# A decode kernel's tail: half rows of the result on 8 neighbouring partitions, odd weight rows summed apart, one plain store, and other cuts of the last weight load

## The chip, the cores and the metric

The kernel runs on one core of a Trainium2 chip. The metric is the device time in microseconds (us) of the whole program. The span of a trace, from the first to the last instruction, is 1.7 to 1.8 us shorter than the time of the same execution (211.0 against 212.7 for the kernel before). All positions "at 207.73" below are microseconds from the start of the span in the trace that is named.

The engines are called PE (matmul), PEld (PE's weight loads), DVE (vector), ACT (scalar), POOL and SP (which issues most of the DMAs).

## The reference

Four tokens go through a layernorm; its result feeds an attention block over a window of 2048 cached keys (16 key heads, 32 query heads of 128) and an MLP block. The results are added.

```python
xn = layernorm(A_x)                                   # 4 x 576
out = A_x + attention(xn, K, V, wq) @ wo              # wo: 4096 x 576
          + xn + gelu(layernorm(xn) @ w3) @ w4        # w3: 576 x 4608, w4: 4608 x 576
# (in the MLP block the shifted terms are zero for a sequence of one token)
```

All inputs are bf16. About 87 MB of cache and weights are read once; there is little arithmetic per byte.

## The kernel before

The result, 4 x 576, is summed in one PSUM tile `acc` in two halves of 288 columns: half `i` in the 32-partition group `i`, batch `b` at partition `32 i + 8 b`. The stationary operands (`gT`, `op`, `idz`) are 32 columns wide with zeros between the four batches. All of `x + xn`, the attention projections (`o_proj`, once per 4 heads) and the MLP's second matmul (`mlp_out`) are added into it without ever resetting it.

```python
    W4_PIECES = [0, 10, NFH, NFH + 10, NFH + 14, NF]

    def load_w4():
        t = wp.tile([P, NF, D], BF16, tag="w", name="w4_sb")
        for lo, hi in zip(W4_PIECES, W4_PIECES[1:]):
            e = lo // NFH
            src = B_w4[e * (F // 2):(e + 1) * (F // 2), :].rearrange("(p i) n -> p i n", i=NFH)
            nc.sync.dma_start(out=t[:, lo:hi, :], in_=src[:, lo - e * NFH:hi - e * NFH, :])
        w_tiles["w4"] = t
    ...
    RS = QD // B
    acc = ps_acc.tile([P, CW], F32)
    nc.vector.memset(acc[:], 0.0)
    ...
    def acc_matmuls(lhsT, rhs):
        for i in range(2):
            nc.tensor.matmul(out=acc[i * QD:(i + 1) * QD, :], lhsT=lhsT, rhs=rhs[:, i * CW:(i + 1) * CW],
                             start=False, stop=False, skip_group_check=True)
    ...
    def o_proj(h):
        if h % WOQ < WOQ - 1:
            return
        for i in range(WOR):
            acc_matmuls(op[:, i, :], wo_tiles[h // WOQ][:, i, :])
    ...
    def mlp_out(lo, hi):
        w4 = w_tiles["w4"]
        for i in range(lo, hi):
            acc_matmuls(gT[:, i, :], w4[:, i, :])
```

`w4` is issued last of all loads, so its pieces also land last. The end of the program, after the last K and V tiles (`hl` is the last head):

```python
    for s in range(NSL):
        pv(hl, s)
    o_scale(hl)
    o_turn(hl - 1)
    o_sum(hl - 1)
    pieces = list(zip(W4_PIECES, W4_PIECES[1:]))
    mlp_out(*pieces[0])
    o_turn(hl)
    o_sum(hl)
    o_spread(hl)
    o_pick(hl)
    mlp_out(*pieces[1])
    o_proj(hl)
    for lo, hi in pieces[2:]:
        mlp_out(lo, hi)

    fin = const.tile([2 * QD, CW], out.dtype)
    nc.vector.tensor_copy(out=fin[:], in_=acc[0:2 * QD, :])
    nc.sync.dma_start(out=o2.rearrange("b (i n) -> i b n", i=2), in_=fin[0:2 * QD:RS, :])
```

PE executes its instructions in this order. The first piece of `w4` stands in front of the last head's transposes (`o_turn(hl)`), and the last head's projection stands in front of the later pieces.

## Time and profile before

| what | where it is read | value |
|---|---|---|
| time | 212.67 us, median of 3 runs | 212.56 to 212.80 |
| bytes read, rate over the span | page, part 3 | 87.17 MB, 413 GB/s |
| share of DMA in the chain that ended last | page, part 4 | 67% |
| last load landed, PE, DVE, store issued | chain, timeline | 206.99, 0.68 us, 0.45 us, 208.21 |
| from the store's issue to the end of the span | 211.0 - 208.21 (spans are given to 0.1 us) | 2.79 us |

The page's slices (40 of 5.3 us each; a digit is the busy share in tenths) show the DMA engines at nine tenths or more from the second slice until the last:

```profile
PEclk9999579799859655957999669999998596969998
DMA  7999999999999999999999999999999999999990
```

The chain that ended last, in order of time (start, length, what; only its end):

```profile
180.05 26.94 DMA w_sb<-in_B_w_dram
206.99 0.04 issue
207.03 0.68 PE acc L314 x8
207.71 0.02 issue
207.73 0.45 DVE fin L601
```

So the program ends with a load, eight matmuls that were waiting for it, an eviction and the store. The timeline of the same stretch (start, length, engine, line, operation, output<-inputs, shapes, count, and in brackets the idle time before it and what ended it):

```profile
198.94 1.40 PE L314 MATMUL acc<-w_sb,gT 128*32 128x288 bf16 x20
...
200.27 0.66 PE L400 MATMUL oT<-ident_w,O_sb 128*128 128x128 f32 x4
...
201.59 1.16 PE L314 MATMUL acc<-w_sb,gT 128*32 128x288 bf16 x16
...
202.64 1.16 PE L314 MATMUL acc<-wo_sb,op 128*32 128x288 bf16 x16
...
204.27 2.04 PE L314 MATMUL acc<-w_sb,gT 128*32 128x288 bf16 x28 [0.47 <-DMA w_sb<-in_B_w_dram]
...
207.03 0.67 PE L314 MATMUL acc<-w_sb,gT 128*32 128x288 bf16 x8 [0.72 <-DMA w_sb<-in_B_w_dram]
...
208.21 0.68 SPq L602 DMA_DIRECT2D out_dram<-fin  x1
```

The first piece (rows 0 to 10 of `w4`, 20 matmuls) starts at 198.94 with no wait, the head's work fills the time until 203.8 (204.27 - 0.47), and PE then waits twice for a load. PE has slack; the loads do not.

### The profile page before, as it was taken

What the parts mean: (1) busy time and instruction counts of PE and PEld (TensorE: products, weight loads), DVE (VectorE), ACT (ScalarE), POOL (GpSimd) and SP (SyncE); (2) the same over time, 40 slices, a digit from 0 to 9 for tenths busy, and PEclk for the clock granted to TensorE, in tenths of its full rate; (3) what the DMA queues carried; (4) which work ended last, traced back from release to release, by engine and by line L of the source; (5) the groups of instructions that cost most, each with busy time, mean ns of one, the idle gap of its engine ahead of it and who ended that gap; (6) DMA issues with size and microseconds to landing.
All of it is one profiled execution on the core that took longest, in us unless ns stands there. A gap on an engine that the chain in (4) does not pass through costs nothing.

```text
span 211.0 us, 2402 instructions
## 1 busy us (share of the span) xinstructions
PE 150.4 (71%) x955; PEld 62.2 (29%) x955; DVE 121.3 (57%) x216; ACT 33.9 (16%) x63; POOL 2.8 (1%) x15
## 2 busy tenths in 40 slices
PE   0386695869395009669999499968693967898982
PEld 0122232224132003214454144334240322433561
DVE  4832989485731082825725968985867284763220
ACT  7703101021102000202121121120211020202300
POOL 4010000000000000000000000000000000000000
PEclk9999579799859655957999669999998596969998
DMA  7999999999999999999999999999999999999990
GB/s 246 435 413 441 422 441 410 443 435 413 450 419 426 438 419 429 434 444 432 416 438 435 416 427 437 435 432 424 436 426 426 420 444 435 422 429 429 425 382 30
DMA packets 6797, 87.32 MB, mean 414 GB/s; under 512 B 758, under 2 KB 770, under 8 KB 1282
## 3 DMA queue, kind: packets, MB, share of 16 engines
q1 hardware_dynamic: 6778, 87.17, 97.2%
q8 instruction: 7, 0.11, 0.2%
q14 instruction: 4, 0.03, 0.0%
q10 hardware_dynamic: 8, 0.00, 0.0%
HBM read 87.17 MB, written 0.00 MB: 413 GB/s over the span
## 4 chain that ended last, share of the span: by engine, by line
DMA 67%; PE 18%; DVE 7%; issue 4%; ACT 1%; SPq 1%; POOL 0%; POOLq 0%; DVEq 0%
DMA w_sb<-in_B_w_dram 29%; DMA vn<-in_A_v_cache_dram 26%; DMA kn<-in_A_k_cache_dram 12%; PE S L335 9%; DVE kt L215 3%; PE g_ps L453 2%; PE q_ps L277 2%; PE O L387 2%; PE oT L400 1%; PE acc L314 1%; DMA first<-in_A_x_dram 1%; DVE qz L309 1%; PE gT_ps L465 1%; DVE mx L341 1%; PE S L357 1%
## 5 line engine op out<-in xcount | busy, mean ns | idle before, releaser
L335 PE MATMUL S<-kt,qz 128*128 128x512 bf16 x256 | 82.0, 452 | 3.1 <-DVE kt L215 3.1
L215 DVE STREAM_TRANSPOSE kt<-kn 128x1024 int32<-128x1024 int32 x64 | 76.8, 1221 | 10.3 <-DMA kn<-in_A_k_cache_dram 9.4
L387 PE MATMUL O<-vn,PT 128*32 128x512 bf16 x256 | 27.8, 434 | 38.5 <-DMA vn<-in_A_v_cache_dram 36.9
L335 PEld LDWEIGHTS <-qz 128*128 128x128 bf16 x256 | 22.2, 106 | 43.2 <-issue 28.5
L363 ACT ACTIVATE E<-S 128x512 bf16<-128x512 f32 x16 | 9.5, 597 | 123.4 <-PE S L357 123.4
L387 PEld LDWEIGHTS <-PT 128*32 128x32 bf16 x256 | 7.3, 95 | 47.2 <-DVE kt L215 23.8
L369 DVE STREAM_TRANSPOSE PT<-E 128x512 bf16<-128x512 bf16 x16 | 11.4, 711 | 14.3 <-ACT E L363 14.3
L353 DVE TENSOR_REDUCE nm<-mg 8x1 bf16<-8x16 f32 x16 | 2.5, 154 | 20.3 <-PE mg L348 20.2
L394 ACT ACTIVATE O_sb<-O,rd 128x512 f32<-128x512 f32 x16 | 11.0, 687 | 16.5 <-issue 11.0
L410 DVE TENSOR_REDUCE on<-oT 128x8 bf16<-128x128 f32 x16 | 4.6, 286 | 15.7 <-PE oT L400 15.7
L400 PE MATMUL oT<-ident_w,O_sb 128*128 128x128 f32 x64 | 11.8, 315 | 0.0
L341 DVE TENSOR_REDUCE mx<-S 128x1 f32<-128x512 f32 x16 | 10.5, 658 | 1.3 <-PE S L335 1.3
L400 PEld LDWEIGHTS oT<-ident_w,O_sb 128*128 128x128 f32 x64 | 9.6, 167 | 5.4 <-issue 3.9
L357 PE MATMUL S<-nm,j_row 8*128 8x512 bf16 x16 | 6.9, 431 | 0.0
L373 PEld LDWEIGHTS dn<-rs,same_j 128*128 128x128 f32 x32 | 5.8, 188 | 2.9 <-ACT E L363 0.7
L326 PE MATMUL S<-negbig,ohT 4*128 4x512 bf16 x16 | 6.2, 385 | 0.0
L314 PE MATMUL acc<-w_sb,gT 128*32 128x288 bf16 x72 | 5.3, 287 | 1.2 <-DMA w_sb<-in_B_w_dram 1.2
L348 PE MATMUL mg<-dm,sel_jb 128*8 128x16 bf16 x16 | 2.8, 175 | 3.7 <-DVE dm L343 3.7
L348 PEld LDWEIGHTS <-sel_jb 128*8 128x8 bf16 x16 | 1.3, 83 | 12.6 <-issue 6.7
L453 PE MATMUL g_ps<-w_sb,ln2T 128*32 128x512 bf16 (+1 forms) x50 | 4.9, 443 | 0.0
L314 PE MATMUL acc<-wo_sb,op 128*32 128x288 bf16 x64 | 4.6, 287 | 0.0
L373 PE MATMUL dn<-rs,same_j 128*128 128x1 f32 x32 | 4.6, 212 | 0.0
(89 smaller groups left out, 72.8 us busy)
## 6 DMA issues: line engine op xcount, KB each, us to landing
kn<-in_A_k_cache_dram SPq DMA_DIRECT2D x16, 2048.0 KB, 22.3
vn<-in_A_v_cache_dram SPq DMA_DIRECT2D x16, 2048.0 KB, 23.9
wo_sb<-in_A_wo_dram SPq DMA_DIRECT2D x4, 1152.0 KB, 25.8
w_sb<-in_B_w_dram SPq DMA_DIRECT2D x2, 2304.0 KB, 31.4
wq_sb<-in_A_wq_dram SPq DMA_DIRECT2D x2, 2048.0 KB, 9.6
w_sb<-in_B_w_dram SPq DMA_DIRECT2D x2, 1440.0 KB, 29.2
w_sb<-in_B_w_dram SPq DMA_DIRECT2D x3, 576.0 KB, 30.5
w_sb<-in_B_w_dram SPq DMA_DIRECT2D x1, 1152.0 KB, 28.7
```

The source lines that it names most:

```text
L215: nc.vector.transpose(out=kt[:], in_=src)
L314: nc.tensor.matmul(out=acc[i * QD:(i + 1) * QD, :], lhsT=lhsT, rhs=rhs[:, i * CW:(i + 1) * CW], start=False, stop=False, skip_group_check= ...
L335: nc.tensor.matmul(out=S_ps[h][:], lhsT=qz[:, z0:z0 + P], rhs=kt[:, ib, :, e:2 * QD:2].rearrange("p c k -> p (c k)"), start=False, stop=Fa ...
L341: nc.vector.reduce_max(out=mx[:], in_=S_ps[h][:], axis=AX.X)
L357: nc.tensor.matmul(out=S_ps[h][:], lhsT=j_row[:], rhs=st.pop(("nm", h))[:, 0:1].to_broadcast([NJ, NW]), start=False, stop=False, skip_grou ...
L363: nc.scalar.activation(out=E[h][:].rearrange("p c k -> p (c k)"), in_=S_ps.pop(h)[:], func=ACT.Exp, scale=scale, accum_out=rs[:])
L369: nc.vector.transpose(out=PT[h][:], in_=E.pop(h)[:])
L373: nc.tensor.matmul(out=dn[:], lhsT=same_j[:], rhs=st.pop(("rs", h))[:], start=True, stop=True)
L387: nc.tensor.matmul(out=O_ps[h][g * QD:(g + 1) * QD], lhsT=PT[h][:, c, :], rhs=vn[:, :, c, :], start=(s == 0), stop=False, skip_group_check ...
L394: nc.scalar.activation(out=O_sb[h][:], in_=O_ps.pop(h)[:], func=ACT.Copy, scale=st.pop(("rd", h))[:, 0:1])
L400: nc.tensor.transpose(out=oT[:, s, :], in_=o[:, s, :], identity=ident_w[:, s * NJ:s * NJ + P])
L453: nc.tensor.matmul(out=g_ps[g * QD:(g + 1) * QD], lhsT=ln2T[:, k, :], rhs=rhs, start=(j == 0), stop=False, skip_group_check=True)
```

## The change

Its intent: the result's half rows (batch 0 half 0, batch 0 half 1, ...) go to 8 neighbouring partitions, so that the store is one plain 8 x 288 copy. For this the stationary operand becomes 10 columns wide with batches at columns 1, 3, 5, 7; half 0 takes columns 1 to 8 and half 1 columns 0 to 7, which shifts its rows by one partition. Both halves then land in one column group, so, to keep two groups running, the even weight rows go to group 0 and the odd ones to group 1. Group 1's sum is copied out by ACT before the last four rows, which go to group 0 alone, and DVE adds it at the end. The first half of `w4` is loaded in one piece, and the last piece is two rows instead of four.

```diff
-    W4_PIECES = [0, 10, NFH, NFH + 10, NFH + 14, NF]
+    W4_PIECES = [0, NFH, NFH + 10, NFH + 14, NF - 2, NF]
 ...
+    OR = 2 * B
+    OW = OR + 2
+    gT = cleared([P, NF, OW], "gT")
+    op = cleared([P, WOR, OW], "op")
 ...
+    def acc_matmuls(terms, nq=2):
+        for i in range(2):
+            for n, (lhsT, rhs) in enumerate(terms):
+                q = n % nq
+                nc.tensor.matmul(out=acc[q * QD:q * QD + OR, :], lhsT=lhsT[:, 1 - i:1 - i + OR],
+                                 rhs=rhs[:, i * CW:(i + 1) * CW], start=False, stop=False, skip_group_check=True)
 ...  (o_proj and mlp_out now take two rows at a time; idz, op and gT are written at columns 1:9:2)
-        for i in range(lo, hi):
-            acc_matmuls(gT[:, i, :], w4[:, i, :])
+        for i in range(lo, hi, 2):
+            acc_matmuls([(gT[:, i + u, :], w4[:, i + u, :]) for u in range(2)], 2 if hi <= NF - 4 else 1)
 ...
-    for lo, hi in pieces[2:]:
+    mlp_out(*pieces[2])
+    odd = const.tile([OR, CW], F32)
+    nc.scalar.activation(out=odd[:], in_=acc[QD:QD + OR, :], func=ACT.Copy)
+    for lo, hi in pieces[3:]:
         mlp_out(lo, hi)
 
-    fin = const.tile([2 * QD, CW], out.dtype)
-    nc.vector.tensor_copy(out=fin[:], in_=acc[0:2 * QD, :])
-    nc.sync.dma_start(out=o2.rearrange("b (i n) -> i b n", i=2), in_=fin[0:2 * QD:RS, :])
+    fin = const.tile([OR, CW], out.dtype)
+    nc.vector.tensor_tensor(out=fin[:], in0=acc[0:OR, :], in1=odd[:], op=ALU.add)
+    nc.sync.dma_start(out=o2.rearrange("b (i n) -> (b i) n", i=2), in_=fin[:])
```

PE's order is not touched: `mlp_out(*pieces[0])`, now 18 rows, still stands in front of `o_turn(hl)`.

## The prediction

> **What bounds it now.** The loads. The page's slices show the DMA engines at nine tenths or more until about 205 of 211.0 us (87 MB at 413 GB/s). The chain of waits ends: last w4 load landed 206.99, 8 PE matmuls 0.68, DVE copy of the accumulator 0.45 (starts 207.73), store issued 208.21 (issue 0.68 us), then 2.1 us to the end. The change touches only this tail; nothing before 198 us should move.
>
> **Where the w4 pieces land** (issue times plus time to landing): rows 0-10 at 198.1, 10-18 about 200.7, 18-28 at 204.2, 28-32 at 205.6, 32-36 at 207.0. In the timeline PE runs the first piece at 198.94 without waiting, then the last head's transposes (200.27), its spread (201.31), the second piece (201.59, while DVE masks and picks until 202.60), the projection (202.64), and from 203.5 waits only on loads.
>
> **What the change does.**
> 1. Rows 0-18 in one load: nothing of it is usable before about 200.7. PE's order is unchanged, so these 36 matmuls stand in front of the last head's transposes, and PE idles from 198.94 to 200.7. Their spacing in the trace is 58 ns (20 in 1.40 us, each 286 ns long). Estimate from these durations: transposes at 203.0, reduced by 204.0, rows 18-28 at 204.3, projection 205.5 to 206.45, rows 28-32 until 207.2. PE's slack is lost, and PE, not the last load, ends the chain.
> 2. New ACT copy of the odd sums, 8x288: about 0.42 us, worked out from the 128x512 copies (0.6-0.69 us). In the built program the first matmul of rows 32-34 waits for it: 207.2 to 207.7.
> 3. Rows 32-36 go to one column group only. [...] eight take 1.13 us, until 208.85. The smaller last piece would help only if the load still ended the chain.
> 4. DVE add instead of copy: 0.43-0.45, the same (a 4x576 float add took 0.73). It starts near 208.9 instead of 207.73: **+1.15 us**.
> 5. Store as 8x288 instead of 2x4x288: [...] the issue should fall from 0.68 towards the 0.33-0.58 of other issues. **-0.25 us** (estimate).
> 6. Smaller clears on ACT, seed matmuls one after the other (some 0.6 us more): off the chain, PE waits for the second layernorm until 12.3.
>
> **Sum:** 212.67 + 1.15 - 0.25 = **213.5 us**, 8 in 10 within 212.3 to 214.4. Faster by over 2%: 0.01; within 2%: 0.96; slower: 0.03.
>
> **What would show it.** Right: PE idle for 1.5-2 us near 199, waiting for a w4 load; the last chain made of PE work from about 200.8 on, with ACT's copy in it; the last load lands near 207 and nobody waits for it; DVE add near 208.9; a shorter store issue. Wrong on 1: PE's last wait is still for w4, DVE add below 208. Wrong on 3: spacing near 60 ns in rows 32-36.
>
> **What would make it wrong.** The first half landing earlier (198-199.5) as one transfer; a throttled clock in the tail after PE's idle (the trace has stretches at 0.50 after pauses), a microsecond or more; a much cheaper store; small last pieces delaying the last landing.

The 1.13 us are part of the +1.15 of step 4, and the sum came to 212.67 + 1.15 - 0.25 = 213.5 us.

## The result, and the profile after

| | before | after |
|---|---|---|
| median us | 212.70 (5 runs) | 215.33 (5 runs) |
| lowest to highest | 212.56 to 212.80 | 213.33 to 215.93 |
| all runs | | 213.33, 215.33, 215.84, 215.93, 215.00 |

The ratio is 1.0113, with a 95% interval from 1.0081 to 1.0144. (Ratios here are the mean time of one kernel's fast runs over that of the other's of the same rounds, so they are not quite the ratio of the medians.) All runs count as fast: on one core the limit for a slow run is 1.5% above the fastest, and these are 1.2% above. But the spread is new: 2.6 us where the kernel before has 0.24.

The one trace at hand was of the shortest execution, 213.33 us. Its chain (start, length, what):

```profile
171.03 29.61 DMA w_sb<-in_B_w_dram
...
200.68 2.37 PE acc L183 x36
...
204.37 2.81 PE acc L183 x42
...
207.21 0.41 ACT odd L600
...
207.66 1.16 PE acc L183 x8
...
208.91 0.45 DVE fin L605
```

The last load is no longer in it; from 200.68 on it is PE's work, with ACT's copy in the middle. The timeline of the same trace:

```profile
200.68 2.37 PE L183 MATMUL acc<-w_sb,gT 128*8 128x288 bf16 x36 [1.93 <-DMA w_sb<-in_B_w_dram]
...
202.98 0.66 PE L401 MATMUL oT<-ident_w,O_sb 128*128 128x128 f32 x4
...
204.30 1.39 PE L183 MATMUL acc<-w_sb,gT 128*8 128x288 bf16 x20
...
206.51 0.66 PE L183 MATMUL acc<-w_sb,gT 128*8 128x288 bf16 x8
...
207.66 1.14 PE L183 MATMUL acc<-w_sb,gT 128*8 128x288 bf16 x8 [0.49 <-ACT odd L600]
...
209.38 0.37 SPq L606 DMA_DIRECT2D out_dram<-fin  x1
```

Up to here every step is where the prediction had put it: the wait for the large load ends at 200.68 (foretold 200.7), ACT copies at 207.21 (207.2), DVE adds at 208.91 (208.9). Only the store is cheaper than foretold: 211.5 - 209.38 = 2.12 us from issue to end, against 2.79. So a short execution is explained, and four of the five executions are not: they are 1.7 to 2.6 us longer than this one.

### The profile page after: what moved, and what is told of

The parts are those of the page before. It is cut to its first block, busy times and chain, and to the rows that moved or that the text cites. A ratio compares the mean times of both kernels' runs of the same rounds, so it can differ in the third digit from the quotient of the medians.

```text
span 211.5 us, 2390 instructions
## 1 busy us (share of the span) xinstructions
PE 146.3 (69%) x941; PEld 61.2 (29%) x955; DVE 120.8 (57%) x216; ACT 33.9 (16%) x64; POOL 2.7 (1%) x15
## 4 chain that ended last, share of the span: by engine, by line
DMA 58%; PE 25%; DVE 9%; issue 5%; ACT 1%; SPq 1%; POOL 0%; POOLq 0%; DVEq 0%
DMA w_sb<-in_B_w_dram 30%; DMA vn<-in_A_v_cache_dram 27%; PE S L336 10%; DVE kt L223 4%; PE acc L183 3%; PE O L388 3%; PE g_ps L454 2%; PE q_ps L283 2%; PE oT L401 2%; DVE mx L342 1%; PE S L358 1%; DMA first<-in_A_x_dram 1%; PE gT_ps L466 1%; DVE qz L315 1%; ACT q_sb L294 1%
## 5 line engine op out<-in xcount | busy, mean ns | idle before, releaser
L336 PE MATMUL S<-kt,qz 128*128 128x512 bf16 x242 | 77.6, 444 | 5.0 <-DVE kt L223 3.1
L401 PE MATMUL oT<-ident_w,O_sb 128*128 128x128 f32 x64 | 11.1, 303 | 0.1
L401 PEld LDWEIGHTS oT<-ident_w,O_sb 128*128 128x128 f32 x64 | 9.1, 160 | 4.8 <-issue 2.7
L183 PE MATMUL acc<-w_sb,gT 128*8 128x288 bf16 x72 | 5.6, 286 | 2.4 <-DMA w_sb<-in_B_w_dram 1.9
L358 PE MATMUL S<-nm,j_row 8*128 8x512 bf16 x16 | 6.4, 398 | 0.0
L183 PEld LDWEIGHTS <-gT 128*8 128x8 bf16 x72 | 3.6, 87 | 3.9 <-issue 2.8
L183 PE MATMUL acc<-wo_sb,op 128*8 128x288 bf16 x64 | 4.6, 286 | 0.0
```

The costliest lines, as they stand in the source:

```text
L183: nc.tensor.matmul(out=acc[q * QD:q * QD + OR, :], lhsT=lhsT[:, 1 - i:1 - i + OR], rhs=rhs[:, i * CW:(i + 1) * CW], start=False, stop=Fals ...
L336: nc.tensor.matmul(out=S_ps[h][:], lhsT=qz[:, z0:z0 + P], rhs=kt[:, ib, :, e:2 * QD:2].rearrange("p c k -> p (c k)"), start=False, stop=Fa ...
L358: nc.tensor.matmul(out=S_ps[h][:], lhsT=j_row[:], rhs=st.pop(("nm", h))[:, 0:1].to_broadcast([NJ, NW]), start=False, stop=False, skip_grou ...
L401: nc.tensor.transpose(out=oT[:, s, :], in_=o[:, s, :], identity=ident_w[:, s * NJ:s * NJ + P])
```

## The experiments

Theory A: the pause of PE near 199, which the change makes, lowers the granted TensorE clock, and as PE's work of the tail is now the chain, the low clock is paid in full. Its base is the trace of the kernel before, where stretches at a clock of 0.50 begin in or soon after pauses of PE: at 90.36 us in a pause of 3.98 us, at 162.04 in one of 3.40, at 175.69 after one of 3.14, at 185.93 after one of 1.45. Theory B: in the long executions the loads (the large first one, or the small last ones) land late. Theory C, which is named in the next text: it was that chip or that moment.

### The changed kernel again

No edit.

> The changed kernel again, unaltered, to see the spread. In its five earlier runs one took 213.33 us (the profiled one, whose tail went as predicted: DVE add at 208.91) and four took 215.0 to 215.9. Theory A (clock): after PE's idle of 2 us near 199 the granted clock falls to 0.5 in most executions, and the matmuls of the tail, about 5.6 us of them, take up to twice as long: again one kernel with runs from 213.3 to 216, and a slow one would show the clock at 0.5 somewhere between 200 and 209 us with the landing of the first w4 load unchanged near 200.7. Theory B (loads): in the slow runs the loads land some 2 us later (the big first one, or the small last ones): the clock of the tail stays 1.0 and the landings move. Theory C: it was that chip or that moment, and the runs now agree near 213.3.

Measured: median 215.01 us, 213.52 to 215.92 in 6 runs (213.52, 215.07, 215.92, 214.93, 215.09, 214.96), ratio 1.0101 [1.0076, 1.0126]. The spread came again (Theory C falls); of 11 executions 9 are at 214.9 or more. The trace was again the shortest execution.

### Two more looks, to catch a long execution

No edit; one execution each.

> The changed kernel once more for one look, to catch the trace of a long execution (215 to 216 us), which the two traces so far are not. If it is long, theory A says: first w4 load lands near 200.7 as in the others, the granted clock is 0.5 for about 3.4 us or more between 200 and 209, the 36 matmuls take about 3.9 us instead of 2.37 (as in the trace of the one-load kernel), DVE add near 210.5. Theory B: clock 1.0, late landings. If it is short, nothing is learnt.

> A third look at the changed kernel, with the same purpose and the same expectations as the look before it.

Measured: 216.09 and 215.13 us, so both traces are of long executions. Below, the busy times by stretch (stretch, its length, then busy us and count of PE, PEld, DVE, ACT and POOL; then granted clock, DMA share, GB/s): first the trace of 213.52 us, then the one of 216.09, then the one of 215.13.

```profile
core 0 of [0], span 211.7 us
...
197.60:200.80 3.20, 0.00 (x0) 0.00 (x0) 0.18 (x1) 0.05 (x1) 0.00 (x0) 1.00 0.98 411
200.80:202.80 2.00, 1.91 (x32) 1.50 (x33) 0.00 (x0) 0.00 (x0) 0.00 (x0) 1.00 0.97 411
202.80:204.80 2.00, 1.62 (x26) 1.07 (x24) 0.47 (x2) 0.00 (x0) 0.00 (x0) 1.00 0.98 399
```

```profile
core 0 of [0], span 214.3 us
...
197.60:200.80 3.20, 0.00 (x0) 0.00 (x0) 0.22 (x1) 0.09 (x1) 0.00 (x0) 0.84 0.96 404
200.80:202.80 2.00, 1.90 (x18) 1.06 (x19) 0.00 (x0) 0.00 (x0) 0.00 (x0) 0.50 0.95 403
202.80:204.80 2.00, 2.00 (x20) 1.16 (x18) 0.00 (x0) 0.00 (x0) 0.00 (x0) 0.50 1.00 410
```

```profile
core 0 of [0], span 213.3 us
...
197.60:200.80 3.20, 0.00 (x0) 0.00 (x0) 0.20 (x1) 0.07 (x1) 0.00 (x0) 1.00 0.95 400
200.80:202.80 2.00, 1.90 (x26) 1.37 (x27) 0.00 (x0) 0.00 (x0) 0.00 (x0) 0.80 0.95 404
202.80:204.80 2.00, 2.00 (x17) 1.14 (x14) 0.00 (x0) 0.00 (x0) 0.00 (x0) 0.50 1.00 408
```

In all three PE idles from about 197.5 to 200.9 and the DMA columns agree. The clock does not: 1.00 throughout in the short execution, 0.50 in the long ones. The first matmuls after the pause, in the timelines of the same three traces (213.52, 216.09, 215.13 us):

```profile
200.89 2.37 PE L183 MATMUL acc<-w_sb,gT 128*8 128x288 bf16 x36 [3.45 <-DMA w_sb<-in_B_w_dram]
```

```profile
200.90 4.49 PE L183 MATMUL acc<-w_sb,gT 128*8 128x288 bf16 x36 [3.41 <-DMA w_sb<-in_B_w_dram]
```

```profile
200.90 3.48 PE L183 MATMUL acc<-w_sb,gT 128*8 128x288 bf16 x36 [3.44 <-DMA w_sb<-in_B_w_dram]
```

They start within 0.01 us of each other, so the large load is not late. Nor are the small last ones: in the longest execution the last of them was issued at 180.1 and landed 26.9 us later, at 207.0, and PE came to the rows of the last two pieces only at 210.45, where it waited for ACT and not for a load:

```profile
210.45 1.14 PE L183 MATMUL acc<-w_sb,gT 128*8 128x288 bf16 x8 [0.49 <-ACT odd L600]
```

So Theory B falls. The 36 matmuls take 2.37, 4.49 and 3.48 us. The transposes behind them take another 0.45 us longer (1.11 and 1.12 instead of 0.66), and DVE's add starts at 209.12, 211.70 and 210.69. These two groups account for the whole delay: 2.12 + 0.45 of the 2.58 us, and 1.11 + 0.46 of the 1.57.

With narrow stretches the moments at which the clock changes can be read to within 0.1 us. In the nine traces that were read so (before, the four of the changed kernel, and the runs filler, merged_only, split and reorder below) every change of the clock that was read lies on a grid of 3.413 us of its own execution, to 0.01 us, and the clock is 1.00 or 0.50. The grid, continued from one change, divides an execution into intervals of 3.41 us and tells the three traces apart. That of the 213.52 us trace cuts the pause at 199.23, so one interval still had 1.6 us of work before the pause and the next 1.75 us after it: no change. In the 215.13 us trace the interval from 198.59 to 202.00 had the pause in its first 2.31 us, and the clock halves at 202.00 for one interval. In the 216.09 us trace the interval from 196.38 to 199.79 had it in its last 2.3 us; the clock halves at 199.79 for two intervals. In the first trace after (213.33 us) PE came later, at 198.75, and of its interval (198.70 to 202.11) 1.9 us were idle: no change.

It would be tempting to put the boundary between 1.9 and 2.3 us of idle in an interval of 3.41. The traces do not allow it. In the kernel before, the interval from 182.52 to 185.93 had 1.96 us of PE work, more than any of these, and the clock halved at 185.93. In the run with two stores below, the interval from 192.58 to 195.99 had 2.52 us of work and no gap above 0.72 us, and the clock halved at 195.99 (worked out from its mean of 0.72 over 197.60 to 200.80, so full again at 199.40, less 3.41; its 16 matmuls from 195.92 on took 1.88 us, in the trace of 213.52 us 1.05); in the trace of 213.52 us an interval with nearly the same instructions and also 2.52 us (192.40 to 195.81) left it at 1.00. None of these intervals was idle throughout. So in these traces the outcome goes with where the pause lies in the grid and with the lack of work, but PE's busy time as the profile counts it does not decide alone. What does is open. The way back to 1.00 is open as well: in the 216.09 us trace the first interval at 0.50 held 2.3 us of PE work and a second one followed; in the 215.13 us trace and the traces of merged_only and reorder it held 2.7 us or more, and there was only the one.

### The pause filled with dummy matmuls

```diff
+    busy = ps_acc.tile([P, NW], F32, tag="g", name="busy")
+    for u in range(9):
+        nc.tensor.matmul(out=busy[:], lhsT=sel_wo[:, 0]..., rhs=sel_wo[:, 0:4]..., start=True, stop=True)
     mlp_out(*pieces[0])
```

> The changed kernel with 9 dummy matmuls of 128x512 (about 1.9 us at full clock) in the place where PE waits for the first w4 load, into a PSUM bank that is free by then; nothing reads them. Theory A (clock): PE does not go idle, the clock stays up, all runs near 213.3 (213.1 to 213.8), little spread. Theory B (loads late): no help, 213.3 to 216 with the same spread as the changed kernel.

Measured: 213.39 us, 213.34 to 213.51 in 5 runs, ratio 1.003 [1.0018, 1.0042]. Nine useless matmuls (1.89 us in the trace, where eight of them are recorded) make the kernel 1.6 us faster at the median (215.01 in the same batch) and remove the spread. In its trace, by stretch as above:

```profile
197.60:200.80 3.20, 3.15 (x30) 1.43 (x19) 0.29 (x1) 0.69 (x1) 0.00 (x0) 1.00 0.96 410
200.80:202.80 2.00, 2.00 (x35) 1.57 (x36) 0.00 (x0) 0.00 (x0) 0.00 (x0) 1.00 1.02 419
```

This is Theory A's number, and the cleanest measure of the change at full clock: +0.6 us. The five times carry this, not the trace alone: in the traced execution PE came at 198.9, as in the short one of 213.33 us.

### One load for the half, and nothing else

The edit to the kernel before, and the same with the nine dummy matmuls of the last experiment:

```diff
-    W4_PIECES = [0, 10, NFH, NFH + 10, NFH + 14, NF]
+    W4_PIECES = [0, NFH, NFH + 10, NFH + 14, NF]
```

> The kernel before with one edit: rows 0 to 18 of w4 in one load instead of two (the last pieces, the two column groups and the old store stay). Counted at full clock from the trace, PE is through its tail at about 207.6 and DVE starts near 207.7, as before: 212.7 us. Theory A: most runs fall into a low clock in the tail and take 214 to 215.5, with a spread of 1 us or more. Theory B with the big load as the culprit: also slower, but with late landings at full clock. Theory B with the small last pieces as the culprit: 212.7, no spread.

> The kernel before with rows 0 to 18 of w4 in one load and the 9 dummy matmuls in PE's pause, nothing else: what the one load costs when the clock stays up. Theory A: the order alone uses up PE's slack exactly: 36 matmuls from 200.75, the last matmul of rows 32 to 36 ends near 207.7, DVE copy at 207.7 to 207.9, 212.75 to 212.95 us and a spread under 0.3 us; the rest of the 214.1 us median of that kernel without dummies is the clock. If the one load costs more than slack at full clock: 213.2 or more.

Measured: without dummies 214.13 us, 212.85 to 215.79 in 6 runs, ratio 1.0068 [1.0035, 1.0101]; with them 212.79 us, 212.71 to 212.88 in 5 runs, ratio 1.0003 [0.9989, 1.0017]. Both are as Theory A foretold, but for one execution below the 214 to 215.5 us of the first and one above. The timelines, without and with dummies:

```profile
200.82 3.89 PE L314 MATMUL acc<-w_sb,gT 128*32 128x288 bf16 x36 [3.42 <-DMA w_sb<-in_B_w_dram]
...
209.37 0.45 DVE L601 CAST fin<-acc 64x288 bf16<-64x288 f32 x1 [2.41 <-PE acc L314]
```

```profile
200.89 2.38 PE L314 MATMUL acc<-w_sb,gT 128*32 128x288 bf16 x36
...
207.93 0.45 DVE L605 CAST fin<-acc 64x288 bf16<-64x288 f32 x1 [2.41 <-PE acc L314]
```

At full clock the one load is free: it uses up the slack of the tail (DVE starts at 207.93; in the kernel before at 207.73) and no more. Its whole cost is the clock, 1.3 us at the median (214.13 - 212.79; the runs are of two batches, with 212.78 and 212.74 for the kernel before). In both chains PE's last 52 matmuls run into DVE's copy without a wait for a load, so PE ends the chain already here.

### The changed kernel with the half in two loads

```diff
-    W4_PIECES = [0, NFH, NFH + 10, NFH + 14, NF - 2, NF]
+    W4_PIECES = [0, 10, NFH, NFH + 10, NFH + 14, NF - 2, NF]
```

(and the calls of the pieces shifted by one, so that rows 0 to 10 stand in front of the last head's transposes, as before).

> The changed kernel with rows 0 to 18 again in two loads (10 and 8), so that PE has work at 199; all else of the change stays. Theory A: no idle, full clock, the last load ends the chain again; DVE add near 207.9, the store's tail 2.14 instead of 2.82 us as in the changed kernel's trace: 212.1 to 212.4, spread of 0.3 us. Theory B with the small last pieces as the culprit: still 2 us of spread, up to 215.

Measured: 212.58 us, 212.40 to 212.59 in 5 runs, ratio 0.9988 [0.9976, 1.0000]. No spread. The time is at the edge of the upper end foretold (212.4) and a little over it. One part of the expectation failed: the last load does not end the chain. The last matmuls wait for ACT's copy:

```profile
206.69 1.14 PE L183 MATMUL acc<-w_sb,gT 128*8 128x288 bf16 x8 [0.49 <-ACT odd L601]
207.94 0.45 DVE L606 TENSOR_TENSOR fin<-acc,odd 8x288 bf16<-8x288 f32 x1 [5.67 <-PE acc L183]
```

So the copy and the one column group cost some 0.2 us until DVE (207.94 against 207.73), and the store gives back more. All of the rest of the change is thus worth -0.2 us (212.58 - 212.78; by the interval between -0.5 and 0), and the one load turns it into +2.2 (215.01 - 212.78).

### PE's order changed, the one load kept

```diff
-    mlp_out(*pieces[0])
     o_turn(hl)
     o_sum(hl)
     o_spread(hl)
     o_pick(hl)
-    mlp_out(*pieces[1])
+    mlp_out(*pieces[0])
     o_proj(hl)
+    mlp_out(*pieces[1])
```

> The changed kernel with its large first load and all else kept, but with PE's order changed: the last head's transposes, spread and pick first, then rows 0 to 18, then the projection, then rows 18 to 28. So what waits for the large load no longer stands in front of work that is ready. If it was the order that cost the slack (my prediction's step 1, the estimate): PE does the transposes at about 199.0, is idle in short pieces only until 200.7, runs rows 0 to 18 until 202.8, projection to 203.8, then waits for 18 to 28 at 204.2; DVE add near 207.95 and 212.5 us with a spread under 0.4 us, as with the half in two loads. If a large load in itself harms (late landing, or a pause that still lowers the clock): 213.5 or more, or spread of 1 us.

Measured: 213.62 us, 212.32 to 213.77 in 6 runs, ratio 1.0028 [1.0009, 1.0047]. The expectation failed for five of six runs; the sixth, 212.32, is what was foretold. The order gives back 1.4 us of the 215.01 (another batch), but PE still idles 1.75 us at a stretch before the load, and the clock still drops. In the trace (213.69 us), by stretch and then in the timeline:

```profile
197.60:200.80 3.20, 1.17 (x14) 0.81 (x13) 1.43 (x4) 0.37 (x1) 0.00 (x0) 0.95 0.93 391
200.80:202.80 2.00, 1.63 (x15) 0.93 (x15) 0.00 (x0) 0.00 (x0) 0.00 (x0) 0.50 1.02 434
```

```profile
201.17 3.69 PE L183 MATMUL acc<-w_sb,gT 128*8 128x288 bf16 x36 [1.75 <-DMA w_sb<-in_B_w_dram]
```

The interval of the grid that ended at 200.49, where the clock halved, had 1.7 us of PE work in it, more than the 1.5 and 1.6 us after which the clock stayed at 1.00 in the tails of 213.33 and 213.52 us; but nearly all of it was transposes and small matmuls. Whether that is the reason no run here tests, and it stays open.

### The shape of the store

On the kernel with the half in two loads, rows in the order (half, batch) on the same 8 partitions, so that the store must be 2x4x288 again:

```diff
-    OW = OR + 2
+    OW = OR + B
-    lhsT=lhsT[:, 1 - i:1 - i + OR]           # batches at columns 1:9:2
+    lhsT=lhsT[:, (1 - i) * B:(1 - i) * B + OR]   # batches at columns 4:8
-    out=o2.rearrange("b (i n) -> (b i) n", i=2), in_=fin[:]
+    out=o2.rearrange("b (i n) -> i b n", i=2), in_=fin[:]
```

> The kernel with the half in two loads (212.58 us), with the 8 half rows on the same 8 neighbouring partitions but in the other order (half, batch) instead of (batch, half), so that the one store has to be written as 2x4x288 as in the kernel before. All else stays. My reading (the shape of the store counts[...]): the issue takes 0.68 us again instead of 0.37, from issue to the end of the span 2.7 to 2.8 us instead of 2.15, and 213.1 to 213.3 us. Rival (neighbouring instead of strided partitions count): 212.6, issue 0.37.

Measured: 213.08 us, 212.98 to 213.26 in 5 runs (at the lower edge of what was foretold), ratio 1.0012 [0.9999, 1.0024], against 212.58 (other batch; 212.78 and 212.75 for the kernel before in the two). The store lines of the timelines, 8x288 and 2x4x288:

```profile
208.41 0.37 SPq L607 DMA_DIRECT2D out_dram<-fin  x1
```

```profile
208.61 0.80 SPq L607 DMA_DIRECT2D out_dram<-fin  x1
```

From issue to the end of the span that is 210.6 - 208.41 = 2.19 and 211.4 - 208.61 = 2.79 us, the latter that of the kernel before within the rounding of the spans. The partitions are the same, so it is the way the store is written that counts, not strided against neighbouring partitions. One thing was changed along with the shape: the 8x288 store writes the result's rows in the order in which they lie in DRAM, the 2x4x288 one does not. No run parts the two.

### Two plain stores on two queues, and two rows in the last piece

On the kernel before:

```diff
-    nc.sync.dma_start(out=o2.rearrange("b (i n) -> i b n", i=2), in_=fin[0:2 * QD:RS, :])
+    for i, eng in enumerate((nc.sync, nc.scalar)):
+        eng.dma_start(out=o2[:, i * CW:(i + 1) * CW], in_=fin[i * QD:(i + 1) * QD:RS, :])
```

and the same with the last four rows of `w4` in two loads of two rows.

> The kernel before with one edit: the store as two plain 4x288 stores, one issued by SP and one by ACT, so that no odd sums, no ACT copy, no add and no matmuls in one column group are needed. If the plain shape is what the change gained: both issues near 0.37 us side by side, the tail after the DVE copy 0.6 us shorter than before: 212.0 to 212.2. If a second store on the other queue costs something of its own at the end: 212.4 to 212.8. No pause of PE, so spread under 0.4 us.

> The same with the last 4 rows of w4 in two loads of 2 rows, both column groups. After the last landing PE then has 4 instead of 8 matmuls, in two groups 0.45 instead of 0.67 us: 0.2 us less, 211.8 to 212.0. If the smaller pieces delay the last landing (near 207.0 so far) the gain is lost: 212.0 to 212.3.

Measured: 213.49 us (213.44 to 213.70), ratio 1.0029 [1.0016, 1.0043], and 213.47 us (213.34 to 213.55), ratio 1.0027 [1.0015, 1.0040]. Both miss. The store lines of the first:

```profile
208.40 0.76 SPq L603 DMA_DIRECT2D out_dram<-fin  x1
208.40 0.70 ACTq L603 DMA_DIRECT2D out_dram<-fin  x1
```

Two stores of 4x288 are both issued as slowly as the old one, and the span ends 3.5 us after the issue (211.9 - 208.40). So a store without a third dimension is not cheap for that alone. Whether it is the four rows, the second queue, or that these rows are not neighbours in DRAM is open. The smaller last piece did what was foretold for PE (0.42 instead of 0.67 us after the landing, DVE at 207.63 instead of 207.92, the landing no later: 207.17 against 207.22 for the first matmul after it), but the two spans differ by 0.2 us and the medians by 0.02, so the gain did not reach the time. (The traced execution of the first, 213.70 us, was its longest; that of the second, 213.47, its median.)

### A version meant to beat both

The half in two loads, the new store, and the odd sums in a PSUM tile of their own in another bank, so that no matmul waits for ACT's copy; only the last two rows in one column group. (The edit is cut to its main lines.)

```diff
-    nc.tensor.matmul(out=acc[q * QD:q * QD + OR, :], ...
+    nc.tensor.matmul(out=accs[q][q * QD:q * QD + OR, 0:CW], ...
+    accs.append(ps_acc.tile([P, NW], F32, tag="g", name="acc1"))   # after the MLP's first matmul
+    nc.vector.memset(accs[1][:], 0.0)
+    mlp_out(*pieces[4])                                            # rows 32 to 34, before the copy
-    nc.scalar.activation(out=odd[:], in_=acc[QD:QD + OR, :], func=ACT.Copy)
+    nc.scalar.activation(out=odd[:], in_=accs[1][QD:QD + OR, 0:CW], func=ACT.Copy)
```

> A version meant to beat both: the half in two loads, the new store, and the odd sums in a PSUM tile of their own in another bank (from the second projection on; cleared once by DVE), so that the matmuls after the ACT copy no longer wait for it; both column groups up to row 34, only the last two rows in one group. After the last landing near 207.05 only 4 matmuls of 120 ns spacing follow: DVE add near 207.75 (the kernel with the half in two loads: 207.94), 212.2 to 212.4 us. If the copy or the last two rows delay it anyway: 212.5 to 212.7. If the projections in one group at first, or the clearing, disturb the middle of the kernel: above 212.8.

Measured: 212.29 us, 212.18 to 212.40 in 5 runs, ratio 0.9979 [0.9967, 0.9992]: as foretold in the time, though DVE's add starts at 207.90 and not at 207.75. It is faster than both kernels, by 0.45 and (across batches) some 2.7 us. Its timeline:

```profile
206.88 0.40 ACT L605 ACTIVATE odd<-acc 8x288 f32<-8x288 f32 x1 [9.26 <-PE acc L184]
207.14 0.65 PE L184 MATMUL acc<-w_sb,gT 128*8 128x288 bf16 x4 [0.30 <-DMA w_sb<-in_B_w_dram]
```

PE now starts the last four matmuls while ACT still copies, and it waits for the load again. The matmuls' wait for ACT in the changed kernel (0.49 us) is a dependency that the built program holds; no run here tried to do without it in one bank, as the other bank was free.

## Why the prediction was right or wrong

It foretold 213.5 us, within 212.3 to 214.4; the median was 215.33.

- **Step 1, the large load and PE's order: right about the chain, wrong about the speed.** PE did wait for the load until 200.7, the slack went, and PE ended the chain. But the sum counted the 36 matmuls, and all that follows, at the 58 ns spacing of the old trace. That spacing was measured at a granted clock of 1.00 (197.60 to 206.80 in the trace before), and the step itself put a pause in front of it. In 11 of 13 executions of the changed kernel the time was 214.9 or more; in the two of them traced the clock was 0.50 for one or two intervals of 3.4 us after or in the pause, and the 36 matmuls took 3.48 and 4.49 instead of 2.37 us. Filling the pause takes 1.6 us away and all of the spread. The prediction named "a throttled clock in the tail after PE's idle" as what could make it wrong, and gave it almost no room: the upper end of the range left 0.9 us, and it was the usual case.
- **The length of the pause** was read from one trace as 1.7 us (198.94 to 200.7). In three of the changed kernel's four traces PE was there at 197.5, and paused 3.4 us, from which the clock halved in two. In the trace of 213.33 us the clock had been halved from 185.04 to 188.46, as in the one of the kernel before (185.93 to 189.34); in the three others it was not, and PE was earlier at its wait and idled for longer. Ten traces, of whatever kernel (the nine above and that of the two stores), divide in this way: where a stretch of halved clock begins between 184.9 and 196 us (five), PE is through the work in front of the first piece of `w4` at 198.7 to 199.0, and where none does (five), at 197.4 to 197.8 (in the reordered kernel: in front of the last head's transposes). So the earlier clock goes with the length of the pause, and the prediction had read that length from one trace.
- **Steps 2 and 3, ACT's copy and one column group: right.** In the trace of 213.33 us 0.40 us for the copy and 1.14 for the eight matmuls (foretold 0.42 and 1.13).
- **Step 4, +1.15 us until DVE: right at full clock:** 208.91 - 207.73 = 1.18.
- **Step 5, the store: right in kind, too small.** Foretold -0.25 us; 2.79 to 2.12 is -0.67 (good to 0.1 us, as the spans are), and undoing the shape alone gave back 0.6 us of tail and 0.5 us of time. About half is the issue (0.68 to 0.37), the rest comes after it. The packets under 512 B after 207.4 us are 2 before and 8 after, 2 again with the 2x4x288 store and 8 with the two stores together. Whether their number has to do with the length of the tail was not tested apart, and why two stores are slower still is not explained by it.
- **Step 6, the start: right.** Nothing of it shows in the time; the kernel with the half in two loads has the same start. (The four seed matmuls took 2.07 us, before 1.17: 0.9 us more, foretold some 0.6.)

The sum at full clock is 1.18 - 0.67 = +0.5, and with the pause filled +0.6 was measured, against +0.9 foretold (1.15 - 0.25); the clock comes on top, with 1.6 us at the median (215.01 - 213.39). The failed step is the first: a duration was carried over from a busy engine to one that the change makes idle.

## What to carry to other kernels

Before you let an engine that has slack wait for a larger load, ask what state it will be in when the load comes: here pauses of PE of 1.75 to 3.4 us were followed by half the clock in four traces, for 3.4 us or twice that, and two others, of 1.9 and 3.45 us, were not. What was slack then becomes the chain at half the clock (36 matmuls: 3.48 to 4.49 us instead of 2.37). A new spread between executions of one kernel was the sign of it here; look at the granted clock of a long execution, not only at the trace that you happen to have. And cut the first piece of a last load to what the engine needs to keep going, or give it other work for the time.

The small stores of these runs, by their shape (bf16, trace of each): 8x288, issue 0.37 us and 2.1 to 2.2 us from issue to the end of the span; 2x4x288, 0.68 to 0.80 and 2.8; two of 4x288 at once on two queues, 0.69 to 0.76 and 3.5 to 3.6.
